# A fused retention and bilinear FFN kernel: transposing k and q with the sync queue's DMA instead of TensorE, from slot 5 on

## The chip, the cores and the metric

The kernel runs on one core of a Trainium2 chip. The metric is the device time of one execution, in microseconds (us); the time of a kernel is the median of several runs. A separate profiled execution gives the trace that is read below: each instruction of each engine with its start and duration, DMA transfers, and what released each wait. Engines are called PE (TensorE, matrix multiply; PEld is its weight load), DVE (VectorE), ACT (ScalarE), POOL (GpSimd) and SP (SyncE, which here only issues DMAs).

## What is computed

A retention recurrence for 4 batches, 8 heads, 768 positions and head dimension 64, then a bilinear feed-forward network (FFN) over the 3072 resulting rows of 512. Inputs and output are float32.

```python
def _attn_ref(q, k, v):                      # q, k, v: (4, 8, 768, 64)
    gamma = 1.0 - 2.0 ** (-5.0 - np.arange(H, dtype=np.float32))
    scale = 1.0 / np.sqrt(D)
    ...
    for t in range(S):
        state = gamma[None, :, None, None] * state + np.einsum('bhd,bhe->bhde', k[:, :, t], v[:, :, t])
        y[:, :, t] = scale * np.einsum('bhd,bhde->bhe', q[:, :, t], state)
    return y

def _moe_ref(x, w_a, w_b, w_out):            # x: (3072, 512), w_a, w_b: (512, 1536), w_out: (1536, 512)
    a = x @ w_a
    b = x @ w_b
    return a * b @ w_out
```

## The kernel before

**Slots.** The rows are cut into 24 slots of 128 positions, six for each batch, with all 8 heads in one slot. For a slot, k and q are scaled by powers of gamma that depend on the position (tables ktab and qtab), which turns the recurrence into ordinary products. Scores of one slot are k times q, masked to the causal half; what comes from earlier slots of the same batch goes through a running state of 64x64 for each head, kept in PSUM and copied to `gst`.

**Work on one slot**, in five pieces:
- `load_slot(t)`, line 81: three DMAs of 256 KB on the sync queue (k, q, v; line 86), into `raw` buffers, six for each.
- `casts(t)`, line 166: scale and cast to bfloat16, mostly on POOL: kb (line 172), qb (line 174), vb (line 145). The `nat` pool has six buffers for each.
- `step_a(t)`, line 178: four PE transposes of kb (line 181) and four of qb (line 183) into one PSUM tile tp, and one DVE copy of it to kqT in SBUF (line 185). The `tra` pool has three buffers.
- `step_b(t)`, line 187: eight matmuls at<-kqT (line 193) for the scores, two DVE products with the mask giving aT (line 197), four matmuls that add the slot to the state (line 203), two ACT copies to gst (line 210).
- `step_c(t)`, line 212: y from state and q (line 218, except for a batch's first slot) and from scores and v (line 223), and one ACT copy of it to xt (line 228), which is the FFN's input, transposed.

**The FFN** works on tiles of 3, 2, 4, 4, 4, 4 and 3 slots (`TILES`). For each tile, `ffn_ab` runs 12 times (4 matmuls for a, line 253; 4 for g, line 259; ACT copies a, line 256; DVE multiplies to ht, line 261), and `ffn_out` once for each slot of the tile (12 matmuls, line 266; ACT copy, line 269; a store of 256 KB on ACT's DMA queue, line 271).

**Order.** `seq` chains the instructions of each engine, SP's DMA issues among them, in the order of the program text. While the FFN of one tile runs, the slots of the next tile are threaded between its pieces by `steps` and `run`: a of slot t, c of slot t-1, b of slot t, each before a given piece of FFN work. `run` calls `casts(t)` when a of slot t is within the next four (three in the first call) entries of the list. Slots 5 to 8 are threaded into the last six `ffn_ab` of the second tile and the five `ffn_out` of the first two tiles (work positions 3 to 10, line 317). From the third tile on the positions are spread evenly (line 325).

**Loads.** The list `LOADS` gives SP's order: slots 0 to 2, then weights between slots 3 and 4, then the output weights o0 to o3, then slots 5 to 23. The first five entries are issued at once, the rest by one call after the first tile's slots (line 306). The DMA issue waits on its buffer, in order.

Of the kernel before, what the change touches and what calls it, by code (L numbers as in the profile page):

```python
# [10 lines left out]
BF16 = mybir.dt.bfloat16  # L11
# [2 lines left out]


TILES = [3, 2, 4, 4, 4, 4, 3]


LOADS = ("s0 s1 s2 w0 w1 s3 w2 s4 w3 o0 o1 o2 o3 "
         + " ".join(f"s{t}" for t in range(5, 24))).split()  # L20


@with_exitstack
def kernel(
# [10 lines left out]
    nc = tc.nc  # L35
    P = 128
    B, H, S, D = q.shape
    NCH = S // P
    HP = H // 2
# [4 lines left out]
    NSLOT = B * NCH  # L44
# [9 lines left out]
    wstage = ctx.enter_context(tc.tile_pool(name="wstage", bufs=4))  # L54
    raw = ctx.enter_context(tc.tile_pool(name="raw", bufs=6))
    nat = ctx.enter_context(tc.tile_pool(name="nat", bufs=6))
    tra = ctx.enter_context(tc.tile_pool(name="tra", bufs=3))
    xtp = ctx.enter_context(tc.tile_pool(name="xtp", bufs=2))
    asbp = ctx.enter_context(tc.tile_pool(name="asbp", bufs=3))
    htp = ctx.enter_context(tc.tile_pool(name="htp", bufs=2))  # L60
# [9 lines left out]
    def seq(bi):  # L70
        ins = bi.ins
        prev = last.get(ins.engine)
        if prev is not None:
            tc.add_manual_dep(ins, prev.name, nosync, reason="program order")
        last[ins.engine] = ins
        return bi
# [4 lines left out]
    def load_slot(t):  # L81
        b, ci = divmod(t, NCH)
        for nm, src in (("k", k), ("q", q), ("v", v)):
            f = raw.tile([P, H, D], F32, tag=nm + "f", name=nm + "f")
            s = src[b, :, ci * P : (ci + 1) * P, :].rearrange("h p d -> p h d")
            seq(nc.sync.dma_start(out=f, in_=s))  # L86
            raws[nm, t] = f
# [16 lines left out]
    def issue_loads(n):  # L104
        for _ in range(min(n, len(pending))):
            what = pending.pop(0)
            {"s": load_slot, "w": load_w, "o": load_o}[what[0]](int(what[1:]))


    issue_loads(5)  # L110
    lgr = const.tile([P, 1, H], F32, name="lgr")
    bq = const.tile([P, 1], F32, name="bq")
# [28 lines left out]
    def cast(engine, dst, src):  # L141
        if engine is nc.scalar:
            seq(nc.scalar.copy(dst, src))  # L143
        else:
            seq(engine.tensor_copy(dst, src))  # L145
# [7 lines left out]
        cast(nc.gpsimd, wo_bf[:, j * FPW : (j + 1) * FPW, :], wst["o", j])  # L153


    kb, qb, vb, kqT, aT = {}, {}, {}, {}, {}
    state = {}
    xt, where = {}, {}
    first = 0
    for J, n in enumerate(TILES):  # L160
        for i in range(n):
# [4 lines left out]
    def casts(t):  # L166
        ci = t % NCH
        early = t < TILES[0]
        kb[t] = nat.tile([P, H, D], BF16, tag="kb", name="kb")
        qb[t] = nat.tile([P, H, D], BF16, tag="qb", name="qb")  # L170
        vb[t] = nat.tile([P, H, D], BF16, tag="vb", name="vb")
        seq((nc.vector if early else nc.gpsimd).tensor_tensor(  # L172
            kb[t], raws["k", t], ktab[:, ci, :, :].to_broadcast([P, H, D]), op=ALU.mult))
        seq(nc.gpsimd.tensor_tensor(  # L174
            qb[t], raws["q", t], qtab[:, ci, :, :].to_broadcast([P, H, D]), op=ALU.mult))
        cast(nc.scalar if early else nc.gpsimd, vb[t], raws["v", t])

    def step_a(t):
        tp = psat.tile([P, 2, HP, P], BF16, tag="at", name="tp")
        for hp in range(HP):  # L180
            seq(nc.tensor.transpose(tp[:, 0, hp, :], kb[t][:, 2 * hp : 2 * hp + 2, :], ident))  # L181
        for hp in range(HP):
            seq(nc.tensor.transpose(tp[:, 1, hp, :], qb[t][:, 2 * hp : 2 * hp + 2, :], ident))  # L183
        kqT[t] = tra.tile([P, 2, HP, P], BF16, tag="kqT", name="kqT")
        seq(nc.vector.tensor_copy(kqT[t], tp))  # L185
# [44 lines left out]
    def steps(slots):  # L230

        slots = list(slots)
        todo = []
        for i in range(len(slots) + 1):
            if i < len(slots):
                todo.append((step_a, slots[i]))
            if i > 0:
                todo.append((step_c, slots[i - 1]))
            if i < len(slots):
                todo.append((step_b, slots[i]))  # L240
        return todo
# [4 lines left out]
    def ffn_ab(J, ft):  # L246
        w = TILES[J] * P
        if ft == 0:
            ht[J] = htp.tile([P, NFT, 4 * P], BF16, tag="ht", name="ht")
        fs = slice(ft * P, (ft + 1) * P)  # L250
        a = psff.tile([P, 4 * P], F32, tag="ff", name="a")[:, :w]
        for kt in range(KT):
            seq(nc.tensor.matmul(a, wa_bf[:, kt, fs], xt[J][:, kt, :w],  # L253
                                 start=(kt == 0), stop=(kt == KT - 1)))
        asb = asbp.tile([P, 4 * P], BF16, tag="asb", name="asb")[:, :w]
        seq(nc.scalar.copy(asb, a))  # L256
        g = psff.tile([P, 4 * P], F32, tag="ff", name="g")[:, :w]
        for kt in range(KT):
            seq(nc.tensor.matmul(g, wb_bf[:, kt, fs], xt[J][:, kt, :w],  # L259
                                 start=(kt == 0), stop=(kt == KT - 1)))  # L260
        seq(nc.vector.tensor_tensor(ht[J][:, ft, :w], g, asb, op=ALU.mult))  # L261

    def ffn_out(J, i):
# [5 lines left out]
        seq(nc.scalar.copy(osb, o))  # L269
        n0 = (sum(TILES[:J]) + i) * P  # L270
        seq(nc.scalar.dma_start(out=out[n0 : n0 + P, :], in_=osb))


    def run(work, todo, at, ahead=4):

        order = []
        for g, w in enumerate(work):
            order += [todo[i] for i in range(len(todo)) if at[i] == g]
            order.append(w)
        starts = [s for fn, s in todo if fn is step_a]  # L280
        for i, (fn, *args) in enumerate(order):
            for fn2, *a2 in order[i : i + ahead + 1]:
                if fn2 is step_a and a2[0] in starts:
                    starts.remove(a2[0])
                    casts(a2[0])
            fn(*args)

    def ab0(ft):
        ffn_ab(0, ft)
        if ft % FPW == FPW - 1 and ft // FPW + 1 < NW:  # L290
            cast_w(ft // FPW + 1)

    casts(0)
    casts(1)
    step_a(0)
    casts(2)
    step_b(0)
    step_a(1)
    step_c(0)
    step_b(1)  # L300
# [12 lines left out]
    work = [(ffn_ab, 1, ft) for ft in range(6, NFT)]  # L313
    work += [(ffn_out, 0, i) for i in range(TILES[0])]
    work += [(ffn_out, 1, i) for i in range(TILES[1])]
    todo = steps(range(5, 9))
# [39 lines left out]
```

## Time and profile before

| | |
|---|---|
| time, median of 3 runs | 255.87 us (255.71 to 256.0) |
| span of the profiled execution, first to last instruction | 254.2 us |
| time of the profiled execution outside its span | not given; the runs' median is 1.64 us above the span |
| granted TensorE clock in the profile, mean | 1.000 |
| PE / DVE / ACT / POOL busy | 233.5 / 102.2 / 91.6 / 73.6 us |
| DMA packets, bytes | 84181, 34.88 MB |
| loads of k, q, v (line 86) | 72, of 256 KB, median 5.1 us from issue to landing |
| output stores | 24, of 256 KB, median 2.1 us from issue to landing |
| transposes, lines 181 and 183 | 96 each, median 219 ns, modelled end |
| kqT copies, line 185 | 24, mean 683 ns |

Rows of a view give microseconds from the span's start. In the order of time a row merges instructions of one line that follow each other (x4, x8): its start, its duration, the engine, the line and the operation, and in square brackets the idle time before it with what ended it. Matmul ends are modelled, and successive matmuls overlap, so what a group costs is read from its start to the next group's start. In the groups the idle time before an instruction is given with what released it. "SPq" marks an issue of a DMA by the sync queue: the duration there is the time that the issue held the queue, not the transfer.

The FFN's tiles from the third on (work of the third to the sixth: 77.44 to 115.35, to 153.55, to 191.30, to 227.05 us; of the seventh: to 250.46 us) are told apart in the trace by their first a matmul.

### The profile page before, as it was taken

How to read it: one execution, taken by the hardware profiler on the slowest of the kernel's cores; microseconds unless marked ns; L12 is line 12 of the kernel's file. 1: busy time of each engine (PE TensorE's matmuls, PEld its weight loads, DVE VectorE, ACT ScalarE, POOL GpSimd, SP SyncE). 2: the span in 40 equal slices, each digit the busy share in tenths (PEclk: the TensorE clock that was granted, in tenths of full speed). 3: DMA queues.
4: the chain of work that ended last, by engine and by line, in shares of the span. 5: the costliest groups of instructions: out<-in, count | busy, mean ns of one | idle time of the engine just before them, and what ended most of it. 6: DMA issues, size and time to landing. Idle time of an engine off the chain costs nothing.

```text
span 254.2 us, 4303 instructions
## 1 busy us (share of the span) xinstructions
PE 233.5 (92%) x1672; PEld 127.0 (50%) x1696; DVE 102.2 (40%) x173; ACT 91.6 (36%) x179; POOL 73.6 (29%) x84
## 2 busy tenths in 40 slices
PE   0487889899999999999999999999999999999994
PEld 0363445786555455445455445445445454446641
DVE  1462375465325456305455306455205465104410
ACT  2154233534243442423434412444314333223311
POOL 5115474286757667503133403000000000000000
PEclk9999999999999999999999999999999999999999
DMA  7999997999999999969910021000021000120012
GB/s 155 219 358 289 303 292 257 296 217 205 252 239 271 209 214 220 191 173 274 183 32 3 3 112 55 0 0 3 24 100 44 0 0 3 41 97 27 3 41 84
DMA packets 84181, 34.88 MB, mean 137 GB/s; under 512 B 75457, under 2 KB 79553, under 8 KB 84161
## 3 DMA queue, kind: packets, MB, share of 16 engines
q1 hardware_dynamic: 80704, 28.32, 50.1%
q10 hardware_dynamic: 3456, 6.29, 6.7%
q8 instruction: 13, 0.21, 0.4%
q14 instruction: 8, 0.06, 0.1%
HBM read 28.31 MB, written 6.29 MB: 136 GB/s over the span
## 4 chain that ended last, share of the span: by engine, by line
PE 88%; SPq 3%; DMA 2%; ACT 2%; DVE 2%; issue 2%; DVEq 0%; ACTq 0%
PE g L259 25%; PE a L253 25%; PE o L266 24%; PE y L223 3%; PE at L193 3%; SPq L86 3%; PE st L203 3%; DMA vf<-in_v_dram 2%; PE tp L181 2%; PE tp L183 2%; PE y L218 2%; DVE wb_bf L145 1%; ACT gst L210 1%; ACT wa_bf L143 1%; ACT xt L228 0%
## 5 line engine op out<-in xcount | busy, mean ns | idle before, releaser
L261 DVE TENSOR_TENSOR ht<-g,asb 128x512 bf16<-128x512 f32 (+2 forms) x84 | 51.6, 615 | 86.8 <-PE g L259 69.2
L253 PE MATMUL a<-xt,wa_bf 128*128 128x512 bf16 (+2 forms) x325 | 76.6, 354 | 2.7 <-ACT xt L228 2.3
L259 PE MATMUL g<-xt,wb_bf 128*128 128x512 bf16 (+2 forms) x332 | 76.5, 353 | 2.6 <-DVE wb_bf L145 2.5
L256 ACT CAST asb<-a 128x512 bf16<-128x512 f32 (+2 forms) x84 | 44.0, 524 | 70.6 <-PE a L253 56.1
L266 PE MATMUL o<-wo_bf,ht 128*128 128x512 bf16 x279 | 63.5, 379 | 0.6 <-issue 0.2
L259 PEld LDWEIGHTS <-wb_bf 128*128 128x128 bf16 x336 | 33.0, 99 | 33.5 <-DVE wb_bf L145 3.6
L266 PEld LDWEIGHTS <-ht 128*128 128x128 bf16 x288 | 27.4, 98 | 31.6
L253 PEld LDWEIGHTS <-wa_bf 128*128 128x128 bf16 x336 | 30.7, 99 | 24.6 <-issue 2.7
L197 DVE TENSOR_TENSOR aT<-at,mask 128x512 bf16<-128x512 f32 x48 | 30.7, 681 | 7.0 <-PE at L193 7.0
L172 POOL TENSOR_TENSOR kb<-kf,ktab 128x512 bf16<-128x512 f32 x21 | 21.9, 1042 | 37.0 <-DMA kf<-in_k_dram 16.7
L185 DVE COPY kqT<-tp 128x1024 bf16<-128x1024 bf16 x24 | 16.4, 683 | 38.4 <-PE tp L183 38.4
L269 ACT COPY osb<-o 128x512 f32<-128x512 f32 x24 | 14.0, 585 | 46.7 <-PE o L266 36.7
L174 POOL TENSOR_TENSOR qb<-qf,qtab 128x512 bf16<-128x512 f32 x24 | 25.0, 1042 | 11.7 <-DMA qf<-in_q_dram 11.2
L210 ACT CAST gst<-st 64x256 bf16<-64x256 f32 x40 | 14.6, 366 | 15.5 <-PE st L203 15.1
L228 ACT CAST xt<-y 128x512 bf16<-128x512 f32 x24 | 14.0, 585 | 15.9 <-PE y L223 13.4
L145 POOL CAST vb<-vf 128x512 bf16<-128x512 f32 x21 | 13.5, 644 | 20.9 <-issue 14.9
L181 PE MATMUL tp<-ident,kb 128*128 128x128 bf16 x96 | 10.0, 230 | 5.0 <-DVE kb L172 5.0
L223 PE MATMUL y<-aT,vb 128*64 128x128 bf16 x192 | 11.1, 235 | 2.1 <-DVE aT L197 2.1
L193 PE MATMUL at<-kqT 64*128 64x128 bf16 x192 | 10.2, 230 | 2.5 <-DVE kqT L185 2.0
L181 PEld LDWEIGHTS <-kb 128*128 128x128 bf16 x96 | 7.7, 103 | 9.1 <-DVE kb L172 5.0
L193 PEld LDWEIGHTS <-kqT 64*128 64x128 bf16 x192 | 5.8, 98 | 10.5 <-issue 7.1
L183 PE MATMUL tp<-ident,qb 128*128 128x128 bf16 x96 | 10.0, 231 | 0.9 <-POOL qb L174 0.9
(28 smaller groups left out, 68.0 us busy)
## 6 DMA issues: line engine op xcount, KB each, us to landing
kf<-in_k_dram SPq DMA_DIRECT2D x24, 256.0 KB, 5.1
qf<-in_q_dram SPq DMA_DIRECT2D x24, 256.0 KB, 5.1
vf<-in_v_dram SPq DMA_DIRECT2D x24, 256.0 KB, 5.1
out_dram<-osb ACTq DMA_DIRECT2D x24, 256.0 KB, 2.1
wsta<-in_moe_w_a_dram SPq DMA_DIRECT2D x4, 768.0 KB, 6.5
wstb<-in_moe_w_b_dram SPq DMA_DIRECT2D x4, 768.0 KB, 7.6
wsto<-in_moe_w_out_dram SPq DMA_DIRECT2D x4, 768.0 KB, 7.3
```

Source lines behind the costliest of these rows:

```text
L172: seq((nc.vector if early else nc.gpsimd).tensor_tensor(kb[t], raws["k", t], ktab[:, ci, :, :].to_broadcast([P, H, D]), op=ALU.mult))
L174: seq(nc.gpsimd.tensor_tensor(qb[t], raws["q", t], qtab[:, ci, :, :].to_broadcast([P, H, D]), op=ALU.mult))
L181: seq(nc.tensor.transpose(tp[:, 0, hp, :], kb[t][:, 2 * hp : 2 * hp + 2, :], ident))
L193: seq(nc.tensor.matmul(at[e][:, hp, :], kqT[t][r, 0, hp, :], kqT[t][r, 1, hp, :], start=True, stop=True))
L197: seq(nc.vector.tensor_tensor(aT[t][:, e], at[e], mask, op=ALU.mult))
L210: seq(nc.scalar.copy(g[r, :, r], st[r, :, r]))
L223: seq(nc.tensor.matmul(y[r, hp, :], vb[t][:, 2 * hp + e, :], aT[t][:, e, hp, :], start=(ci == 0 and hp == 0), stop=(hp == HP - 1), skip_gr ...
L253: seq(nc.tensor.matmul(a, wa_bf[:, kt, fs], xt[J][:, kt, :w], start=(kt == 0), stop=(kt == KT - 1)))
L256: seq(nc.scalar.copy(asb, a))
L259: seq(nc.tensor.matmul(g, wb_bf[:, kt, fs], xt[J][:, kt, :w], start=(kt == 0), stop=(kt == KT - 1)))
L261: seq(nc.vector.tensor_tensor(ht[J][:, ft, :w], g, asb, op=ALU.mult))
L266: seq(nc.tensor.matmul(o, ht[J][:, ft, i * P : (i + 1) * P], wo_bf[:, ft, :], start=(ft == 0), stop=(ft == NFT - 1)))
```

## The change

Slots 0 to 4 stay as they are. From slot 5 on, `step_a` returns without doing anything. In its place `flip(t)`, called at the end of `casts(t)`, issues one DMA on the sync queue that transposes eight 128x128 blocks of bfloat16 from SBUF to SBUF, from kb and qb straight into kqT. For this kb and qb become the two halves of one tile kqb. The `tra` pool has four buffers in place of three, for kqT and for aT. The load list ends with slot 10; from slot 5 on `casts(t)` issues, after its flip, the loads of slot t+6.

```diff
+ON_PE = 5
...
 LOADS = ("s0 s1 s2 w0 w1 s3 w2 s4 w3 o0 o1 o2 o3 "
-         + " ".join(f"s{t}" for t in range(5, 24))).split()
+         + " ".join(f"s{t}" for t in range(5, 11))).split()
...
-    tra = ctx.enter_context(tc.tile_pool(name="tra", bufs=3))
+    tra = ctx.enter_context(tc.tile_pool(name="tra", bufs=4))
...
+    def flip(t):
+        kqT[t] = tra.tile([P, 2, HP, P], BF16, tag="kqT", name="kqT")
+        seq(nc.sync.dma_start_transpose(out=kqT[t].rearrange("p a b c -> p (a b) c"),
+                                        in_=kqb[t].rearrange("p a h d -> p (a h d)")))
...
     def casts(t):
         ci = t % NCH
         early = t < TILES[0]
-        kb[t] = nat.tile([P, H, D], BF16, tag="kb", name="kb")
-        qb[t] = nat.tile([P, H, D], BF16, tag="qb", name="qb")
+        kqb[t] = nat.tile([P, 2, H, D], BF16, tag="kqb", name="kqb")
+        kb[t], qb[t] = kqb[t][:, 0], kqb[t][:, 1]
         vb[t] = nat.tile([P, H, D], BF16, tag="vb", name="vb")
...
         cast(nc.scalar if early else nc.gpsimd, vb[t], raws["v", t])
+        if t >= ON_PE:
+            flip(t)
+            if t + 6 < NSLOT:
+                load_slot(t + 6)
 
     def step_a(t):
+        if t >= ON_PE:
+            return
         tp = psat.tile([P, 2, HP, P], BF16, tag="at", name="tp")
```

More of the change, by code (lines that the diff above doesn't have):

```diff
@@ L107, in issue_loads @@
             {"s": load_slot, "w": load_w, "o": load_o}[what[0]](int(what[1:]))
+    def flip(t):
+        kqT[t] = tra.tile([P, 2, HP, P], BF16, tag="kqT", name="kqT")
+        seq(nc.sync.dma_start_transpose(out=kqT[t].rearrange("p a b c -> p (a b) c"),
+                                        in_=kqb[t].rearrange("p a h d -> p (a h d)")))
+    kqb = {}
+    kb, qb, vb, kqT, aT = {}, {}, {}, {}, {}
     issue_loads(5)
@@ L153, in cast_o @@
         cast(nc.gpsimd, wo_bf[:, j * FPW : (j + 1) * FPW, :], wst["o", j])
-    kb, qb, vb, kqT, aT = {}, {}, {}, {}, {}
     state = {}
```

## The prediction

> **What bounds the kernel now.** I read the page's busy rows and the chain that ended last first, to find the engine that sets the end.
>
> ```profile
> span 254.2 us, 4303 instructions
> PE 233.5 (92%) x1672; PEld 127.0 (50%) x1696; DVE 102.2 (40%) x173; ACT 91.6 (36%) x179; POOL 73.6 (29%) x84
> PE 88%; SPq 3%; DMA 2%; ACT 2%; DVE 2%; issue 2%; DVEq 0%; ACTq 0%
> ```
>
> TensorE (PE) is 92% busy and carries 88% of the chain; VectorE's kqT copy has no entry of its own in that chain. So a microsecond taken from PE's stream is a microsecond gained, a microsecond in which PE waits is one lost, and time freed on VectorE is worth nothing by itself. The stage rows agree: from 77.44 to 250.46 us PE idles under 0.4 us in each stage.
>
> Next, PE's order of time around slot 5, the first slot that the change touches.
>
> ```profile
> 54.52 0.60 PE L259 MATMUL g<-xt,wb_bf 128*128 128x256 bf16 x4
> 54.96 0.39 PE L181 MATMUL tp<-ident,kb 128*128 128x128 bf16 x4
> 55.18 0.39 PE L183 MATMUL tp<-ident,qb 128*128 128x128 bf16 x4
> 55.40 0.60 PE L253 MATMUL a<-xt,wa_bf 128*128 128x256 bf16 x4
> 55.84 0.60 PE L259 MATMUL g<-xt,wb_bf 128*128 128x256 bf16 x4
> 56.37 0.40 PE L193 MATMUL at<-kqT 64*128 64x128 bf16 x8
> ```
>
> Columns: start, duration, instruction. Ends are modelled, so cost is read from start to start. The eight transposes of a slot hold PE from 54.96 to 55.40, 0.44 us. Only 0.97 us after them PE asks for kqT of slot 5. That is short because the slot's casts have only just been made, as POOL's rows show:
>
> ```profile
> 52.18 1.04 POOL L172 TENSOR_TENSOR kb<-kf,ktab 128x512 bf16<-128x512 f32 x1
> 53.18 1.04 POOL L174 TENSOR_TENSOR qb<-qf,qtab 128x512 bf16<-128x512 f32 x1
> ```
>
> Last, the sync queue's (SP's) order of time. These are the loads of slot 9's v, slot 10 and slot 11's k.
>
> ```profile
> 63.90 1.69 SPq L86 DMA_DIRECT2D vf<-in_v_dram  x1
> 65.64 0.85 SPq L86 DMA_DIRECT2D kf<-in_k_dram  x1
> 68.10 0.37 SPq L86 DMA_DIRECT2D qf<-in_q_dram  x1
> 68.51 0.88 SPq L86 DMA_DIRECT2D vf<-in_v_dram  x1
> 72.06 0.37 SPq L86 DMA_DIRECT2D kf<-in_k_dram  x1
> ```
>
> SP issues loads almost without pause from 45.22 us on, about 1.1 us for each 256 KB (line 86 medians 1.06 to 1.09 us), and the DMA engines are saturated (share 1.09 between 45 and 95 us). Slot 10's loads leave SP only at 65 to 69 us. This row decides the case.
>
> **What the change removes.** PE loses 8 transposes in each of 19 slots: 19 x 0.445 us (two groups of 0.22) = 8.5 us, all on the path. VectorE loses 19 copies of 0.683 us, 13.0 us, off the path: nothing. The PSUM buffers of tp come free: nothing, since PE does not wait for them once the stages run full. With no new wait the span would be 254.2 - 8.5 = 245.7 us.
>
> **What it adds: one transfer, "flip", per slot, in SP's order.** In program order the flip of slot 5 stands behind all loads up to slot 10, because the load list still issues slots 5 to 10 at once. An SP queue works in order, so the flip is late whatever it costs itself. Step by step:
> - Slot 10's k is issued by 65.64 + 0.85 = 66.49. Its q then waited until 68.10 in the old trace, which is when slot 5's first output store had landed (68.08). In the new order that store comes after flip 5, so it cannot be waited for. I take 2 x 1.06 us for q and v: flip 5 starts at 68.6 us.
> - A flip moves 256 KB, like a load. The trace shows no transposing transfer, so its cost is bounded by the load rows: queue time 0.37 us (shortest issue) to 3.9 us (longest), issue to landing 3.3 us to 10.5 us (ends of the kf group). I take the median load, 1.1 us and 5.1 us, as flip 5 also stands behind the four or five loads then under way (5.1 / 1.1). It lands at 73.7 us.
> - PE, without slot 5's transposes, asks for it at 56.37 - 0.44 = 55.93 and stands still for 17.8 us; every later PE instruction is queued behind it.
> - After a long halt PE may restart slowly. At the start of the kernel four groups of 128x384 came 1.28 us apart, and later ones 0.65: about 2.5 us lost. No long halt of a warm PE is in this trace, so the bound is 0 to 2.5 us; I take 2.5.
> - From slot 5's scores (56.37) to the first matmul of the next tile (77.44) is 21.07 us now; four slots' transposes (6 to 9) leave it, 1.78 us: 19.3 us, or 21.8 with the slow restart. PE reaches the next tile at 73.7 + 21.8 = 95.5 us, 18.1 us late.
> - Flips 6, 7 and 8 each stand behind one flip and three loads: 4 x 1.1 = 4.4 us apart, landing at 78.1, 82.5 and 86.9. PE wants slot 8 last, about 6.4 us before the next tile, at 89: covered, with 2.2 us to spare.
> - After that the cover is wide. Flip t (from slot 9 on) waits for one of four kqT buffers, that is for y of slot t-4; queued behind it on SP are the loads of slot t+6 and flip t+1. A slot takes about 9 us of PE, so there are some 27 us between that release and its use. Price nothing; if that cover went, each late flip would cost PE its lateness.
> - The loads from slot 11 on now follow flips and casts. POOL's cast of slot t+6 waits for slot t's buffers anyway, and POOL is idle after 160 us: nothing. Merging kb and qb into one tile, and a fourth tra buffer, add no instruction: nothing.
>
> Behind 77.44 us the old profile has 176.8 us, of which 14 slots' transposes go, 6.2 us: 170.6. Sum: 95.5 + 170.6 = 266.1 us of span. The recorded times of three runs have a median of 255.87 us, 1.64 us above this profile's span; no other time of the profiled execution is given, so I carry that offset over: **267.8 us**, 11.9 us slower.
>
> Three rules of the Trainium skill bear on this, and nothing above uses them. "Advanced Engine Details and Errata", section X-Bar Transpose (TRN2), says transposing DMAs are as fast as regular ones, which gives the flip my 1.1 us and the sum above. "VectorE: DVE Perf Modes", The three transpose paths, gives 1309 ns for a 128x128 block on the DMA crossbar against 390 on TensorE (0.055 us per block from start to start in the rows here); eight blocks one after another would be an estimated 10.5 us and rival B's time. "TensorE: Matmul & The Clock Gate", section "Why this matters for your kernels", warns of PE gaps above about 3 us, after which its clock falls to half; that speaks against this change; by it the sum stands with its slow restart, without it the time is 265.3 us.
>
> **Rivals.**
> - A, a flip costs SP three to five microseconds. Then flips 6 to 8 are late too. Slot 8 lands at 72.6 + F + 3 x (3.3 + F), and the next tile starts 6.4 us later, at 88.9 + 4F: with F = 3 the span is 271.5 (273 us), with F = 3.9 it is 275 (277), with F = 5 279.5 (281). It takes over where F passes 1.8 (2.2 us of spare over three flips, on top of 1.1). For it: a transposing write may be cut finer than a load. Against: the load's pieces are small already, 75457 of 84181 packets under 512 B.
> - B, flips as slow as the slowest load, 10.5 us each, become the bound: 72.6 + 19 x 10.5 + 13 slots' loads of 3.3 = 315 us for the last one, and about 40 us of PE work behind slot 23's scores: 355 us. It decides when flip and loads exceed the 9 us of a slot.
> - C, faster: SP gets flip 5 out in time and everything hides: 245.7 + 1.6 = 247.4 us. Place: SP at 54.2 us, when slot 5's q is cast. It comes out faster only if flip 5 lands by about 61.9 us (55.93 + 8.5 - 2.5). At that time SP has issued only up to slot 8's loads, with 6 to 7 us of saturated queue before the flip. For it speaks only that SP's order could differ from the program text; the code chains each engine's instructions in program order.
> - D, the halt is smaller: shortest issues and landing (66.49 + 0.74 + 3.3 = 70.5) and no slow restart: 70.5 + 19.3 + 170.6 = 260.4, that is 262 us.
>
> **How the numbers follow.** Main case with D as its lower end (F up to 2.5): 0.70, 262 to 271 us. A: 0.16. B and anything between 5 and 10.5 us: 0.08. C: 0.05. Anything ending near the old time: 0.01. A measurement of this kernel tells 0.2%, 0.5 us, from no change. Faster 0.05, same 0.01, slower 0.94. The range is 262 to 282 us: it takes in the main case, D's end and A, and leaves out B and C.
>
> **What would show it.** Right: in the changed profile the flip of slot 5 leaves SP after slot 10's v, at 67 to 70 us; PE idles 15 to 20 us before line 193's matmul, released by that DMA; FFN groups just after take about double time; tiles from the third on take 36.1 us in place of 37.9; chain shares of SP and DMA rise. Wrong: PE idle there under 8 us (C), further waits at each slot's scores in later tiles (B), or waits at slots 6 to 8 that add up to more than the first (A).

## The result, and the profile after

The changed kernel takes 268.96 us (median of four runs, 267.62 to 270.33), against 255.94 for the kernel before: 1.050 times as long, 95% interval 1.047 to 1.053. The profiled execution took 268.12 us, with a span of 266.4.

The page of the changed kernel: the span, the busy rows, and the chain by engine and by line.

```profile
span 266.4 us, 3992 instructions
...
PE 229.1 (86%) x1544; PEld 119.7 (45%) x1544; DVE 90.6 (34%) x154; ACT 91.8 (34%) x179; POOL 73.2 (27%) x84
...
PE 69%; SPq 16%; DMA 11%; POOL 2%; issue 1%; ACT 0%; POOLq 0%
```

PE's share of the chain fell from 88% to 69%. The sync queue (SPq, 3% before) and transfers (2% before) now hold 27% of it: the end of the kernel is followed back through one long stretch of load issues. Where the chain, in order of time, comes back to PE, it comes through the flip of slot 6, not through that of slot 5:

```profile
67.03 5.04 DMA vf<-in_v_dram
...
73.00 6.53 DMA kqT<-kqb
79.52 0.04 issue
79.57 0.40 PE at L206 x8
```

PEld shows 152 instructions fewer (1696 before), the 8 x 19 transposes that went.

PE's order of time around slot 5, after the change (line 206 is the scores' matmul, line 193 before; 266 and 272 are a and g):

```profile
55.30 0.60 PE L272 MATMUL g<-xt,wb_bf 128*128 128x256 bf16 x4
72.97 0.60 PE L206 MATMUL at<-kqT 64*128 64x128 bf16 x8 [17.06 <-DMA kqT<-kqb]
73.51 1.04 PE L266 MATMUL a<-xt,wa_bf 128*128 128x256 bf16 x4
74.34 1.06 PE L272 MATMUL g<-xt,wb_bf 128*128 128x256 bf16 x4
75.19 1.06 PE L266 MATMUL a<-xt,wa_bf 128*128 128x256 bf16 x4
...
79.57 0.40 PE L206 MATMUL at<-kqT 64*128 64x128 bf16 x8 [1.47 <-DMA kqT<-kqb]
```

The two brackets hold the main cost: PE stands idle for 17.06 us until the flip of slot 5 lands, and for 1.47 us more until that of slot 6 does. No later flip holds PE up. Between the two waits the FFN groups start 0.83 to 0.85 us apart, where they started 0.44 apart before.

The sync queue's order of time (line 87: loads, here slot 10's k, q, v and slot 11's; line 112: flips 5 to 7):

```profile
64.66 1.14 SPq L87 DMA_DIRECT2D kf<-in_k_dram  x1
65.85 1.14 SPq L87 DMA_DIRECT2D qf<-in_q_dram  x1
67.03 1.14 SPq L87 DMA_DIRECT2D vf<-in_v_dram  x1
68.28 2.25 SPq L112 DMA_TRANSPOSE kqT<-kqb  x1
70.58 0.57 SPq L87 DMA_DIRECT2D kf<-in_k_dram  x1
71.19 0.58 SPq L87 DMA_DIRECT2D qf<-in_q_dram  x1
71.87 1.01 SPq L87 DMA_DIRECT2D vf<-in_v_dram  x1
73.00 2.34 SPq L112 DMA_TRANSPOSE kqT<-kqb  x1
...
78.99 2.29 SPq L112 DMA_TRANSPOSE kqT<-kqb  x1
```

Flip 5 leaves the queue at 68.28 us, straight behind slot 10's v, though POOL had made its operands by 54.5 us, some 14 us earlier.

Four stages of the changed kernel: PE's wait, from slot 5's scores to slot 6's, from there to the next tile, and one full tile. The last three columns are the granted clock, the DMA engines' share and GB/s.

```profile
55.90:72.90 17.00, 0.01 (x1) 0.00 (x0) 0.43 (x1) 0.00 (x0) 13.04 (x15) 0.65 1.21 216
72.97:79.50 6.53, 5.13 (x36) 3.51 (x36) 2.14 (x4) 1.33 (x3) 2.65 (x3) 0.61 1.37 186
79.50:96.09 16.59, 16.52 (x128) 8.29 (x129) 3.87 (x6) 6.20 (x13) 8.04 (x9) 1.00 1.30 233
96.09:132.05 35.96, 35.96 (x233) 16.94 (x232) 13.08 (x20) 13.93 (x26) 10.57 (x12) 1.00 1.26 235
```

The granted clock is 0.61 just after the halt and 1.00 from 79.5 us on. A full tile takes 35.96 us where it took 37.91: the gain is there, 1.95 us in each tile of four slots, and is outweighed by the halt.

### The profile page after: what moved, and what is told of

Its sections match the earlier page's. It is cut to its first block, busy times and chain, and to the rows that moved or that the text cites. A ratio compares the mean times of both kernels' runs of the same rounds, so it can differ in the third digit from the quotient of the medians.

```text
span 266.4 us, 3992 instructions
## 1 busy us (share of the span) xinstructions
PE 229.1 (86%) x1544; PEld 119.7 (45%) x1544; DVE 90.6 (34%) x154; ACT 91.8 (34%) x179; POOL 73.2 (27%) x84
## 4 chain that ended last, share of the span: by engine, by line
PE 69%; SPq 16%; DMA 11%; POOL 2%; issue 1%; ACT 0%; POOLq 0%
PE o L279 24%; PE a L266 19%; PE g L272 18%; SPq L87 15%; DMA wsto<-in_moe_w_out_dram 4%; DMA wsta<-in_moe_w_a_dram 3%; DMA kqT<-kqb 2%; PE y L236 2%; PE at L206 2%; DMA vf<-in_v_dram 2%; PE st L216 2%; SPq L94 2%; PE y L231 1%; POOL wa_bf L153 1%; POOL wo_bf L153 1%
## 5 line engine op out<-in xcount | busy, mean ns | idle before, releaser
L272 PE MATMUL g<-xt,wb_bf 128*128 128x512 bf16 (+2 forms) x336 | 78.3, 357 | 2.5 <-DVE wb_bf L153 2.5
L266 PE MATMUL a<-xt,wa_bf 128*128 128x512 bf16 (+2 forms) x336 | 78.5, 357 | 2.3 <-ACT xt L241 2.3
L279 PE MATMUL o<-wo_bf,ht 128*128 128x512 bf16 x288 | 64.5, 379 | 0.0
L266 PEld LDWEIGHTS <-wa_bf 128*128 128x128 bf16 x336 | 31.8, 100 | 28.6 <-issue 2.7
L179 POOL TENSOR_TENSOR kqb<-kf,ktab 128x512 bf16<-128x512 f32 x21 | 21.9, 1042 | 34.2 <-PE st L216 18.8
L181 POOL TENSOR_TENSOR kqb<-qf,qtab 128x512 bf16<-128x512 f32 x24 | 25.0, 1042 | 7.9 <-DMA qf<-in_q_dram 7.4
L236 PEld LDWEIGHTS <-vb 128*64 128x64 bf16 x192 | 6.9, 116 | 6.2 <-issue 4.4
L216 PE MATMUL st<-vb,kqb 128*128 128x128 bf16 x80 | 8.6, 234 | 0.5 <-ACT gst L223 0.5
L231 PE MATMUL y<-kqT,gst 128*128 128x128 bf16 x80 | 8.5, 233 | 0.0
L231 PEld LDWEIGHTS <-gst 128*128 128x128 bf16 x80 | 6.7, 106 | 3.9
```

Source lines behind the costliest of these rows:

```text
L179: seq((nc.vector if early else nc.gpsimd).tensor_tensor(kb[t], raws["k", t], ktab[:, ci, :, :].to_broadcast([P, H, D]), op=ALU.mult))
L181: seq(nc.gpsimd.tensor_tensor(qb[t], raws["q", t], qtab[:, ci, :, :].to_broadcast([P, H, D]), op=ALU.mult))
L236: seq(nc.tensor.matmul(y[r, hp, :], vb[t][:, 2 * hp + e, :], aT[t][:, e, hp, :], start=(ci == 0 and hp == 0), stop=(hp == HP - 1), skip_gr ...
L279: seq(nc.tensor.matmul(o, ht[J][:, ft, i * P : (i + 1) * P], wo_bf[:, ft, :], start=(ft == 0), stop=(ft == NFT - 1)))
```

## The experiments

The theory (queue): what costs is the place of the first flip in SP's order, behind the loads up to slot 10. Rivals: the transposing transfer is dear by itself, or its traffic is; the loads that moved behind the casts are late; the trouble belongs to slots 5 to 8.

**Loads only three slots ahead.** The flip of slot 5 now stands behind slot 7.

```diff
-         + " ".join(f"s{t}" for t in range(5, 11))).split()
+         + " ".join(f"s{t}" for t in range(5, 8))).split()
...
-            if t + 6 < NSLOT:
-                load_slot(t + 6)
+            if t + 3 < NSLOT:
+                load_slot(t + 3)
```

> The changed kernel, but with the loads only three slots ahead of the flips: the load list ends with slot 7, and the casts of slot t issue the loads of slot t+3 after the flip. Queue theory (flip 5 is late because it stands behind the loads up to slot 10 on SP): it now stands behind slot 7's, which leave SP at 57.6 us, so it lands about 4.6 us later, at 62.2; PE's wait for slot 5 falls from 17.1 us to about 6.3, flips follow 5.7 us apart (2.3 for the flip, 3 x 1.1 for the loads), waits at slots 6 to 8 stay under 3 us together; time 256.5 to 260 us against the changed kernel's 268.1 to 269. Rival (the flip itself is dear: its transfer or its contention costs the time): the wait and the time stay within 3 us of the changed kernel's, 265 us or more.

Measured: 256.93 us (256.13 to 258.86), 1.003 times before (1.0006 to 1.0061). PE's order of time in this kernel:

```profile
62.60 0.61 PE L206 MATMUL at<-kqT 64*128 64x128 bf16 x8 [7.50 <-DMA kqT<-kqb]
...
68.62 0.40 PE L206 MATMUL at<-kqT 64*128 64x128 bf16 x8 [1.74 <-DMA kqT<-kqb]
68.95 0.47 PE L216 MATMUL st<-vb,kqb 128*128 128x128 bf16 x4
69.20 4.41 PE L279 MATMUL o<-wo_bf,ht 128*128 128x512 bf16 x12
```

The same 19 flips, nine load issues fewer ahead of the first: the wait falls from 17.06 to 7.50 us, the time by 12 us. The wait was expected at 6.3; part of the difference is that this run's PE came to it earlier, at 55.1. The last row shows a second slow stretch, after the short wait: twelve matmuls took 4.41 us where they take about 2.7. What set that off, these runs do not show. The profiled execution, 258.86 us, is also the slowest of this kernel's ten; the other nine have higher mean granted clocks (0.977 to 0.987, against 0.973), so the stretch need not be in them.

**The change without flips.** `flip(t)` is left out and all slots are transposed on PE; the loads still follow the casts.

```diff
         if t >= ON_PE:
-            flip(t)
...
     def step_a(t):
-        if t >= ON_PE:
-            return
```

> The changed kernel without any flip: all slots are transposed on TensorE as before, but the loads from slot 11 on are still issued at the casts (t+6), kb and qb are still one tile, tra still has four buffers. Queue theory: these edits cost nothing, within 0.5 us of the kernel before, 255.4 to 256.4 us. Rival (the moved loads are what is late): slower by 2 us or more.

256.01 us, 0.999 (0.997 to 1.001): the moved loads, the merged tile and the fourth buffer cost nothing.

**Flips that nothing reads.** All flips are issued, into an unused tile, and PE transposes every slot.

```diff
-        kqT[t] = tra.tile([P, 2, HP, P], BF16, tag="kqT", name="kqT")
+        idle = tra.tile([P, 2, HP, P], BF16, tag="idle", name="idle")
...
     def step_a(t):
-        if t >= ON_PE:
-            return
```

> The changed kernel with all slots transposed on TensorE as before; every flip is still issued in its place, into a tile that nothing reads. It has all of the flips' traffic and queue time and none of the waits of PE for them. Queue theory: only PE's wait costs, so the time is within 1 us of the kernel before, 255 to 257 us. Rival (the flips' traffic or queue time slows loads and casts enough to cost): 258 us or more.

255.80 us, 0.998 (0.996 to 1.001). The flips' traffic and their queue time, 19 of them in the saturated stretch and after, cost nothing that can be measured. Together with the kernel before this, it leaves only PE's wait for a flip.

**The change's order, from slot 9 on.** If the wait comes from the backlog, it moves with it.

```diff
-ON_PE = 5
+ON_PE = 9
...
-         + " ".join(f"s{t}" for t in range(5, 11))).split()
+         + " ".join(f"s{t}" for t in range(5, 15))).split()
```

> Flips only from slot 9 on, in the change's own order: the load list ends with slot 14, and from slot 9 on the casts of slot t issue the loads of slot t+6 after the flip. Queue theory: the wait moves with the backlog. Flip 9 stands behind slot 14's loads, which left SP at 85.9 us in the old profile, and lands 4.6 us later, at 90.5; TensorE asks for it at 78.8 and waits 11.7 us, with a slow restart of 2.4 us behind it unless another flip hides it; 15 slots x 0.445 = 6.7 us gained: 256 - 6.7 + 11.7 + 2.4 = 263.4, range 259 to 265. Rival (the wait belongs to slots 5 to 8, whose casts are made just before their use): slots 9 and later have their cover, about 249.5 us.

263.42 us (1.030, 1.024 to 1.035). PE's order of time:

```profile
78.14 1.03 PE L272 MATMUL g<-xt,wb_bf 128*128 128x512 bf16 x4
91.20 0.61 PE L206 MATMUL at<-kqT 64*128 64x128 bf16 x8 [12.03 <-DMA kqT<-kqb]
```

Slot 9 waits 12.03 us, with 11.7 expected. So the wait is not bound to slots 5 to 8. The slow restart behind it was smaller than the 2.4 us expected: from slot 9's scores to the first matmul of the next tile PE took 35.62 us here, and 34.15 us in the kernel with loads two slots ahead (below), which has no halt there: 1.5 us more.

**The same order, from slot 13 on.** The list goes to slot 18 (`ON_PE = 13`, `range(5, 19)`).

> Flips only from slot 13 on, in the change's own order (load list to slot 18, then slot t+6 after the flip). Queue theory: flip 13 stands behind slot 18's loads, off SP at about 101 us, and lands at 105.5; TensorE asks for it at about 117, so nothing waits, and 11 slots x 0.445 = 4.9 us are gained: 251.1 us, range 250.5 to 252. Rival (a transfer on the path at every slot): 254 or more.

251.22 us, 0.982 (0.977 to 0.986): no row of PE waits for a flip. Flip 13 left the queue at 101.6 us and landed 5.7 us later; PE asked for it at 117.28. By slot 13 the queue has got ahead of PE, and the change's order does what it says.

**From slot 9 on, loads two slots ahead.** `ON_PE = 9`, the list to slot 10 as in the change, and:

```diff
-            if t + 6 < NSLOT:
-                load_slot(t + 6)
+            if t + 2 < NSLOT:
+                load_slot(t + 2)
```

> Flips only from slot 9 on, slots 5 to 8 on TensorE as before; the load list ends with slot 10, and from slot 9 on the casts of slot t issue the loads of slot t+2 after the flip. Queue theory: flip 9 stands behind slot 10's loads (off SP at about 69.4 us in the old profile) and behind its own cast (69.5), lands at about 74.5, before PE asks for it (79.3); no wait on a flip longer than 1 us; 15 slots x 0.445 = 6.7 us gained: 249.2 us, range 248 to 251. Rival (flip dear by itself): waits at the scores of slots 9 to 12, 253 us or more.

249.54 us, 0.972 (0.969 to 0.976), faster than both kernels. The page, and the stretch around slot 9 on PE:

```profile
span 247.7 us, 4039 instructions
...
PE 226.6 (91%) x1576; PEld 119.3 (48%) x1576; DVE 93.0 (38%) x158; ACT 91.9 (37%) x179; POOL 73.5 (30%) x84
```

```profile
77.22 1.03 PE L266 MATMUL a<-xt,wa_bf 128*128 128x512 bf16 x4
78.08 1.03 PE L272 MATMUL g<-xt,wb_bf 128*128 128x512 bf16 x4
79.04 0.40 PE L206 MATMUL at<-kqT 64*128 64x128 bf16 x8
```

No bracket stands behind slot 9's scores: flip 9, off SP at 71.15 us, landed 4.5 us later. Fifteen slots' transposes are gone from PE, 6.7 us by the prediction's term, and 6.5 us of span are.

**What lies behind the first wait.** Four kernels on one chip ask what the slow restart and the wait for flip 6 cost. First the change again:

> The changed kernel once more, beside the three that follow. 267.6 to 270.4 us, as recorded.

269.47 us (268.1 to 271.24). Then the change with work for PE while it waits:

```diff
     def step_b(t):
         ci = t % NCH
+        if t == 5:
+            fill = psff.tile([P, 4 * P], F32, tag="ff", name="fill")
+            for _ in range(72):
+                seq(nc.tensor.matmul(fill, ident, wa_bf[:, 0, : 4 * P], start=True, stop=True))
```

> The changed kernel, with 72 matmuls of 512 columns (72 x 0.2165 = 15.6 us, into a PSUM tile that nothing reads) ahead of slot 5's scores, so that TensorE is at work while it waits for flip 5 and its clock should not fall. The slow restart disappears in both theories: the FFN groups after slot 5's scores come 0.44 us apart in place of 0.85. Theory S (in the changed kernel the slow restart hides behind the wait for flip 6, which lands at 79.5 us whatever TensorE does): the wait for slot 6 grows from 1.5 to about 3.7 us, and the time stays within 0.6 us of the changed kernel's fast end, 267.2 to 268.4. Rival (the slow restart lies on the path, as the prediction's sum has it): 265.3 to 266.3 us.

268.62 us (1.048, 1.045 to 1.051, against 1.052, 1.046 to 1.058, for the change again). It settles nothing: the filling ended too early, 2.83 us before flip 5, and the restart was slow all the same. A cleaner pair puts flips 5 to 8 together, ahead of the loads of slots 11 to 14:

```diff
-            if t + 6 < NSLOT:
-                load_slot(t + 6)
+            for u in range(11, 15) if t == 8 else [t + 6] * (t > 8):
+                if u < NSLOT:
+                    load_slot(u)
```

> The changed kernel with the flips of slots 5 to 8 issued one behind the other, and the loads of slots 11 to 14 after them: from slot 9 on as in the change. Theory S: flip 6 no longer stands behind a slot's loads and lands by 75.5; the wait at slot 6 goes, and now the slow restart (2.4 us) does lie on the path: next tile at 72.97 + 19.3 + 2.4 = 94.7 in place of 96.1, 1.4 us faster than the changed kernel: 266.3 to 267.6. Rival: the order after flip 5 doesn't matter, within 0.5 us of the changed kernel.

266.50 us (266.32 to 266.82; 1.040, 1.037 to 1.043): all four runs are faster than the fastest of the change again (268.1), so the order after flip 5 does matter, and slot 6's wait is gone. And this with the 72 matmuls:

> The flips of slots 5 to 8 together, as in the kernel before this one, and the 72 matmuls ahead of slot 5's scores. Theory S: with neither a wait for flip 6 nor a slow restart the next tile starts at 72.97 + 19.3 = 92.3, 2.4 us earlier than with the flips together alone: 263.9 to 265.2 us. Rival (no slow restart, or not on the path): the same as with the flips together alone.

265.73 us (1.036, 1.033 to 1.040). From slot 5's scores to the next tile, first with the flips together, then with the filling as well:

```profile
72.35:94.03 21.68, 21.42 (x161) 11.90 (x165) 6.00 (x10) 7.54 (x16) 9.55 (x11) 0.88 1.28 228
```

```profile
72.75:92.03 19.28, 19.01 (x162) 10.53 (x166) 5.91 (x10) 7.52 (x16) 8.30 (x10) 1.00 1.10 235
```

The stage is 2.40 us shorter when PE stays at work, and the clock is 1.00 in place of 0.88: the slow restart is real and costs 2.4 us there. But of these only 0.8 us reached the median, which lies outside the 263.9 to 265.2 us expected, and the two intervals overlap. PE's next rows in the second kernel show where the gain went:

```profile
92.89 1.03 PE L277 MATMUL g<-xt,wb_bf 128*128 128x512 bf16 x4
96.59 0.40 PE L211 MATMUL at<-kqT 64*128 64x128 bf16 x8 [2.67 <-DMA kqT<-kqb]
```

PE comes sooner to slot 9, whose flip now stands behind twelve loads, and waits 2.67 us for it, where the kernel without the filling waits 0.19. In this profiled execution, the slowest of its four (266.79 us), the gain was given back at the next flip.

## Why the prediction was right, point by point

- **Where flip 5 leaves SP**: 68.28 us, 68.6 predicted. Slot 10's q did follow its k at once (65.85), without the wait for the kernel's first output store that it had before. (The medians of line 86 are 1.06 to 1.10 us, not 1.09; nothing hangs on it.)
- **Landing**: PE was released at 72.97, 4.7 us after the issue; the load row's median of 5.1 gave 73.7. All 19 flips took 3.0 to 7.1 us, median 4.6, and the loads of the same profile 4.8 to 5.2 in the median. For the landing the load row was the right neighbour; for the time in the queue it was not (below). X-Bar Transpose (TRN2) in the Trainium skill's "Advanced Engine Details and Errata" fits the landing times; the estimate of 10.5 us worked out from "VectorE: DVE Perf Modes", The three transpose paths, is not seen in any of them.
- **The halt**: 17.06 us, 17.8 predicted.
- **The slow restart**: 2.5 us predicted, 2.40 measured between the last two kernels, at a granted clock of 0.61 in the changed kernel after the halt. "TensorE: Matmul & The Clock Gate", Why this matters for your kernels, agrees for a halt of 17 us. But the sum put it on the path of the changed kernel, and there it was not: all of it lies before 79.57 us, when flip 6 lets PE go (the clock is 1.00 from 79.5 us on), so PE would have waited for flip 6 in its place. This is read from the chain; the run that was to show it, the filling alone, did not.
- **The mis-sized term**: flip 6, "covered". Its scores were to come at 73.7 + 2.8 + 2.5 = 79.0 and its flip to land at 78.1; PE was let go at 79.57. The flip left on time, and that is luck: the queue holds a flip for 2.2 us, not 1.1 (2.170 median, 1.232 at the least), but the first loads behind a flip go out in 0.57 us instead of 1.1, so that it left at 73.00, which is 68.6 + 4.4. What the sum priced too low is its landing, 6.5 us instead of 5.1. Flip 7 left 6.0 us after it, not 4.4. Slots 7 and 8 had no wait, as said, but flip 8 landed at 88.75 and was asked for at 89.68: 0.9 us to spare instead of 2.2.
- **Rival A's limit** was passed: it was to take over where the queue holds a flip for over 1.8 us. With 2.2 its formula puts the next tile at 97.7 us. It did not come to that, because its price per slot, 3 x 1.1 and the flip, was too high: from flip 5 to flip 8 the queue took 5.1 us per slot, not 5.5. Perhaps the transfers ahead of a flip drain while it holds the queue; no run tested that.
- **The next tile**: 96.09 us, 95.5 predicted, and here too luck helped. Slot 6's scores came 6.60 us after slot 5's, against 2.75 in the last kernel, which has neither the restart nor the wait for flip 6. So PE was held 3.85 us for flip 6, and the 2.5 us of restart in the sum stood in its place; flip 5 being 0.7 us early took up part of the rest. The 19.3 us from slot 5's scores to the next tile at full speed are right: the last kernel took 19.28.
- **The rest**: 170.3 us, 170.6 predicted; a tile 35.96, 36.1 predicted. The 0.445 us per slot stand: 251.2 us from slot 13 on and 249.5 from slot 9 on are where it put them.
- **The cover of later flips** held: the change with no flip and with unread flips is the kernel before, and no flip after slot 6 kept PE waiting.

The median is 1.2 us above the prediction, and the profiled execution 0.3. The changed kernel's runs spread over 2.7 us, where the runs before spread by 0.9; its two longest have the two lowest mean granted clocks (0.956 and 0.954, against 0.967 and 0.961). What lowers the clock in some runs was not tried.

## What to carry to other kernels

A DMA that takes over an engine's step takes its place in that queue's order, which this program also fixes by its own chain of issues: count the issues that stand ahead of it and ask when the last of them leaves, before asking what the transfer costs. Here the transfer was cheap, even free where it had time, and its place cost 17 us of waiting. No run issued the flips from another engine's queue; whether that would pass the loads by stays open. Prefetches that are not yet needed belong behind such a transfer, and the step is best moved only from where the queue has got ahead of the consumer: two such versions came out 1.8% and 2.8% faster than the kernel before.

## What the runs showed of the hardware

- A transposing DMA of 256 KB, SBUF to SBUF, held the sync queue 1.23 us when little else was under way (the changed kernel's last seven, from 138 us on) and 2.0 to 3.4 us, median 2.3, among the loads before that. Four in a row, behind loads, held it 6.73 us: 2.33 us the longest of them, 1.23 the shortest.
- How long TensorE stood idle did not alone decide whether it came back slow. After 2.83 us without work (the filled wait that ended too early) FFN groups came 0.82 to 0.86 us apart in place of 0.44, at a granted clock of 0.54; after 2.67 us (slot 9 in the last kernel) they kept their pace and the clock was 1.00; after 1.74 us (loads three slots ahead) twelve matmuls took 4.41 us, at 0.65.
